# Two attention loops with two step tables: in most groups of the second, VectorE makes 20 of 64 score tiles instead of 19

## The chip, the cores and the metric

The kernel runs on one core of a Trainium2 chip. The metric is the device time of one execution in microseconds (us), taken over several runs. A profile of one execution shows what each engine of the core does: PE is TensorE (matrix products; PEld is its weight loads), ACT is ScalarE, DVE is VectorE, POOL is GpSimd, SP issues transfers.

## What is computed

Four residual layers, two kinds in turn, on a sequence of 2048 rows of 512 features:

```python
x = x + _A_ref(_layernorm(x), A_w_r, A_w_i)      # filter in the frequency domain
x = x + _B_ref(_layernorm(x), wq, wk, wv, wo)    # attention, 32 heads, one shared key/value head
x = x + _A_ref(...);  x = x + _B_ref(...)        # the same weights once more

# _B_ref:  q = x @ wq (32 heads of 16);  k = x @ wk (16);  v = x @ wv (16)
scores = jnp.einsum("bhqd,bkd->bhqk", q, k) * (Dh ** -0.5)
o = jnp.einsum("bhqk,bkd->bhqd", _softmax(scores), v);  return o @ wo
```

The two attention layers take most of the time. Each has 32 heads x 2048 x 2048 scores, and every score needs an exponential.

## The kernel before

**Groups and tiles.** An attention layer is one loop (`Attention.run`, from L558; it is called twice, once for each "pair" of a filter and an attention layer, L1053). It goes over 32 groups: 4 query blocks of 512 rows, and 8 sets of 4 heads in each. A group has 64 score tiles (16 blocks of 128 keys x 4 heads), each 128 keys x 512 queries. A tile is made by one product with 32 rows of K (`score`, L673).

**Two ways to an exponential.** Most tiles go to ScalarE, which takes the exponential of two or three tiles in one instruction (`act_step`, L764). The others go to VectorE: one instruction a tile (`dv_pass`, L798, "a pass") multiplies and adds, and the 16-bit integer that comes out is read as a bfloat16, a rough power of two. It is made better by three shifted copies of the same integers ("images"), each with its own weight in the values table. Two images are made by VectorE for a whole batch of tiles at a time (`image_step`, L813), the third by GpSimd, one tile at a time (L817). A VectorE tile thus needs four products with the values, a ScalarE tile one (`pv_step`, L777).

**Steps.** The order of all engines is written out by hand as a list of steps; `chain()` keeps each engine to it. A step is one ScalarE instruction: 3 tiles in even steps, 2 in odd ones (`OPW`, L31 and L585). In a group of the loop 19 tiles are VectorE's, in three batches of 6, 7 and 6 (`DPOS`, L28); 45 are ScalarE's, which makes 18 steps. Group 0 has no first batch, so ScalarE makes 51 tiles there. The second loop has 579 steps in all. `s0[g]` is the first step of group g; steps below are counted from it.

**What one step issues**, in this order (L833 to L851): the score products of ScalarE's tiles and the exponential; the score products of VectorE's tiles (one as a rule, two in a doubled step); on VectorE what is pending (the query cast L489 or the residual add L733 behind a product of the step before), the turning of a finished group (L694), the passes, what is due (reciprocal L699, `qabs` L493, the turning back L715), then an image; on GpSimd its images and the division (L709); then the products with the values, up to a number of rounds of four (`ROUNDS`, L656); and last a "piece": the product of the next group's queries (L483) or, in four groups of a query block, a product with `wo` (L728). VectorE's scores have two banks of PSUM; a piece holds one of them until its result is taken. ScalarE's have one buffer of 3 banks and one of 2.

**GpSimd is paced.** Each of its images and each division waits for the VectorE image issued last (`pace`, L679).

The first loop's row statistics (L150) follow its residual adds; in the second loop the finished rows are sent out instead (L1044). The planner's numbers that the change touches are module constants: `DPOS`, `SHORT`, `TWICE`, `IMG`, `ROUNDS`, `QSTEP`, `OSTEP`, `STAT`, `HOLD`, `QABS` (L28 to L32), and the delays in `evict` and `normalise` (1 step to the reciprocal, 3 to the division, 3 from there to the turning back; L699, L700, L723). Both loops use the same.

Of the kernel before, what the change touches and what calls it, by code (L numbers as in the profile page):

```python
# [470 lines left out]
class Attention:  # L471
# [86 lines left out]
    def run(self, row_done, work, psums):  # L558
# [7 lines left out]
        def chain():  # L566
            traced = nc.cur_bb.bb.instructions
            start = 0
            if mark[0] is not None:
                start = next(k for k in reversed(range(len(traced))) if traced[k] is mark[0]) + 1  # L570
                for i in traced[start:]:
# [6 lines left out]
            mark[0] = traced[-1]  # L578

        NG = NQB * HG  # L580
        ops = []
        stream = [(g, p // 4, p % 4) for g in range(NG) for p in range(64)
                  if not any(p in pos for pos in DPOS[g == 0:])]
# [9 lines left out]
        NS = len(ops)  # L593
        d_score, d_phase = {}, {}
        for g in range(NG):
            for b, pos in enumerate(DPOS):
                if g == 0 and b == 0:
                    continue
                base = s0[g] + BSTEPS * b
                tiles = [(p // 4, p % 4) for p in pos]  # L600
                steps = [base - BSTEPS + k for k in range(BSTEPS) for _ in range(1 + (len(pos) > BSTEPS and k in TWICE[b]))]
                clash = lambda pm: sum(any(u[2] == tiles[i][1] for u in ops[n]) for n, i in zip(steps, pm)) + \
                    sum(tiles[i][1] == tiles[j][1] for n, m, i, j in zip(steps, steps[1:], pm, pm[1:]) if n == m)
                pm = min(itertools.permutations(range(len(pos))), key=clash)
                tiles = [tiles[i] for i in pm]
                for i, n in enumerate(steps):
                    d_score.setdefault(n, []).append((g, b, i) + tiles[i])
                for k in range(BSTEPS):
                    d_phase[base + k] = (g, b, k, tiles)
                s1[g] = max(s1[g], base + BSTEPS - 1)  # L610
        LAG, NBT = 2, max(len(pos) for pos in DPOS)
# [17 lines left out]
        piece_at = {}  # L629

        def place(n0, kind, k):
            n = n0 if n0 % 2 else n0 + 3
            piece_at[n] = (kind, k)

        for g in range(NG - 1):
            place(s0[g] + QSTEP, "q", g + 1)
        for qb in range(NQB - 1):
            for i in range(4):
                place(s0[HG * (qb + 1) + 1 + i] + OSTEP, "o", 4 * qb + i)

        def full_round(queue):
            lst = []
# [6 lines left out]
        for n in range(NS + LAG + 2):  # L649
            queue += due.get(n, [])  # L650
            lst = pv_list[n] = []
            if n in evict_at:
                assert not any(u[0] == evict_at[n] for u in queue)
                continue
            g = evict_at.get(n + 1)
            rounds = 0 if n in piece_at else ROUNDS[n % 2]  # L656
            while queue:
                rnd = full_round(queue if g is None or not any(u[0] == g for u in queue) else [u for u in queue if u[0] == g])
                must = g is not None and any(u[0] == g for u in queue)
                if not must and (rounds <= 0 or len(rnd) < 4 and len(queue) < HOLD):  # L660
# [29 lines left out]
        def evict(g):  # L690

            ps = pv.pop(g)
            o = small.tile([P, 16, 32], F32, tag="oraw")
            nc.vector.transpose(out=o.rearrange("p c j -> p (c j)"), in_=ps)  # L694
# [36 lines left out]
        def residual(k, ps):  # L731
            r, t = (k % 4, k // 4)
            nc.vector.tensor_tensor(out=x_sb[:, r, t, :], in0=ps, in1=x_sb[:, r, t, :], op=ALU.add)  # L733
            if t == NQB - 2:
                n = s0[NG - 3 + r // 2] + (4, 14)[r % 2]
            else:
                n = s0[HG * (t + 1) + 5 + r] + STAT
            later(max(2, n - now[0]), lambda: finish(r, t))

        def finish(r, t):  # L740
# [60 lines left out]
        def image_step(n):  # L801
            if n in d_phase:
                g, b, k, tiles = d_phase[n]
                src, nt = tb[(g, b)].bitcast(I16), len(tiles)
                if k == 0:
                    pool_new = work.tile([P, NBT, 512], I16, tag="SP", bufs=2)
                    sb[(g, b, 3)] = pool_new
                if k in IMG:
                    i = 1 + IMG.index(k)
# [3 lines left out]
                    image[0] = nc.vector.tensor_scalar(out=s_new[:, lo:nt, :], in0=src[:, lo:nt, :], scalar1=PH_OFF[i], scalar2=None, op0=ALU.add)  # L813
                    if lo:
                        pace(nc.gpsimd.tensor_scalar(out=s_new[:, 0:lo, :], in0=src[:, 0:lo, :], scalar1=1.0, scalar2=PH_OFF[i], op0=ALU.mult, op1=ALU.add))
# [4 lines left out]
        def piece(kind, k):  # L820
            ps = psd.tile([P, 512], F32, tag=f"dv{1 - bank[0]}")
            held[0] = ps
            if kind == "q":
                qproj(k, ps)
                pending.append(lambda: QT.__setitem__(k, qcast(ps)))
                later(QABS, lambda: qabs(QT[k]))
            else:
                outproj(k, ps)
                pending.append(lambda: residual(k, ps))
            pending.append(lambda: held.__setitem__(0, None))  # L830

        pending = []
        for n in range(NS + LAG + 2):  # L833
            now[0] = n
            act_step(n)
            dv = dv_score(n)
            for fn in pending:
                fn()
            del pending[:]
# [38 lines left out]
def full_kernel(ctx, tc, A_x, A_w_r, A_w_i, B_x, B_wq, B_wk, B_wv, B_wo, out, n_pairs=2):  # L878
# [135 lines left out]
    for pair in range(n_pairs):  # L1014
# [35 lines left out]
        with ExitStack() as ap:  # L1050
            work = ap.enter_context(tc.tile_pool(name=f"workB{pair}", bufs=2, side="right", reuse_waits="tile"))
            psums = [ap.enter_context(tc.tile_pool(name=f"{n}{pair}", bufs=1, space=PSUM, reuse_waits="tile")) for n in ("psc", "psd", "psp")]
            last = att.run(row_done, work, psums)  # L1053
# [62 lines left out]
```

## Time and profile before

| | us |
|---|---|
| three runs, median (lowest to highest) | 1527.45 (1525.3 to 1530.04) |
| the profiled execution's own time | 1530.11 |
| its span, first to last instruction | 1528.3 |
| first loop, window 107 to 757: DVE, ACT, PE, POOL busy, of 650.0 | 622.02, 646.87, 579.85, 377.17 |
| between the loops, window 757 to 857: DVE, ACT, PE busy, of 100.0 | 90.74, 62.49, 89.81 |
| second loop, window 857 to 1520: DVE, ACT, PE, POOL busy, of 663.0 | 623.62, 658.01, 590.23, 386.43 |

The profile gives an engine's busy time as a union: where two instructions of one engine overlap, the time counts once. A row of its time line reads: start, time, engine, line, operation, result <- inputs, shapes, and how many instructions were merged; in brackets the idle time before it and what ended it. L813 with 128x3072 is an image of six tiles, with 128x3584 one of seven. On VectorE and ScalarE an instruction starts before the one ahead has ended, so what an instruction costs in a full queue is the distance from its start to the next one's, and not its own length.

### The profile page before, as it was taken

How to read it: one execution, taken by the hardware profiler on the slowest of the kernel's cores; microseconds unless marked ns; L12 is line 12 of the kernel's file. 1: busy time of each engine (PE TensorE's matmuls, PEld its weight loads, DVE VectorE, ACT ScalarE, POOL GpSimd, SP SyncE). 2: the span in 40 equal slices, each digit the busy share in tenths (PEclk: the TensorE clock that was granted, in tenths of full speed). 3: DMA queues.
4: the chain of work that ended last, by engine and by line, in shares of the span. 5: the costliest groups of instructions: out<-in, count | busy, mean ns of one | idle time of the engine just before them, and what ended most of it. 6: DMA issues, size and time to landing. Idle time of an engine off the chain costs nothing.

```text
span 1528.3 us, 32995 instructions
## 1 busy us (share of the span) xinstructions
PE 1345.2 (88%) x13152; PEld 427.7 (28%) x13192; DVE 1429.0 (94%) x2283; ACT 1427.3 (93%) x1349; POOL 781.0 (51%) x1310
## 2 busy tenths in 40 slices
PE   5988888899889988999889888889998899889987
PEld 2532222222222222222235322222222222222222
DVE  7888999999999999999989789999999999999996
ACT  4669999999999999999964899999999999999997
POOL 1005555555556555655600155555556655665555
PEclk9988999999999999999999899999999999999999
DMA  8120000000000000000010100000000000000000
GB/s 286 25 42 2 1 2 2 2 1 2 2 2 2 1 2 2 1 2 1 2 47 13 23 2 2 1 2 5 5 2 5 5 5 5 5 5 5 5 5 18
DMA packets 25263, 20.69 MB, mean 14 GB/s; under 512 B 17428, under 2 KB 22548, under 8 KB 24852
## 3 DMA queue, kind: packets, MB, share of 16 engines
q1 hardware_dynamic: 24724, 17.53, 3.9%
q8 instruction: 103, 1.69, 0.5%
q0 software_dynamic: 384, 1.05, 0.2%
q14 instruction: 52, 0.43, 0.1%
HBM read 13.59 MB, written 2.10 MB: 10 GB/s over the span
## 4 chain that ended last, share of the span: by engine, by line
DVE 35%; ACT 34%; issue 14%; PE 11%; POOL 0%; DVEq 0%; POOLq 0%; ACTq 0%
ACT e L764 34%; DVE t_new L798 17%; DVE s_new L813 9%; PE sc L675 3%; PE pv_new L777 3%; DVE o L694 1%; DVE qt L489 1%; DVE ot_new L715 1%; PE dv L675 1%; DVE st L159 1%; PE new L271 1%; PE new L441 1%; DVE qt L493 1%; DVE x_sb L457 0%; PE new L411 0%
## 5 line engine op out<-in xcount | busy, mean ns | idle before, releaser
L764 ACT ACTIVATE e<-sc 128x1536 bf16<-128x1536 f32 (+1 forms) x1158 | 1314.1, 1301 | 5.7 <-PE dv L675 3.6
L817 POOL TENSOR_SCALAR pool_new<-t_new 128x512 int16<-128x512 int16 x1204 | 730.2, 629 | 707.6 <-DVE s_new L813 614.4
L798 DVE TENSOR_SCALAR t_new<-dv 128x512 uint16<-128x512 f32 x1204 | 789.8, 678 | 58.4 <-PE dv L675 51.4
L777 PE MATMUL pv_new<-e,vaug 128*32 128x512 bf16 x2892 | 587.1, 388 | 0.0
L675 PE MATMUL sc<-qt,KT 32*128 32x512 bf16 x2892 | 457.1, 386 | 115.8 <-ACT e L764 110.5
L675 PE MATMUL dv<-qt,KT 32*128 32x512 bf16 x1204 | 452.7, 386 | 18.9 <-DVE t_new L798 15.8
L777 PE MATMUL pv_new<-s_new,vaug 128*32 128x512 bf16 x2408 | 427.7, 386 | 6.7 <-DVE s_new L813 6.2
L813 DVE TENSOR_SCALAR s_new<-t_new 128x3584 int16<-128x3584 int16 (+1 forms) x380 | 393.5, 1036 | 0.1
L675 PEld LDWEIGHTS <-KT 32*128 32x128 bf16 x4096 | 156.0, 91 | 558.3 <-issue 553.4
L777 PE MATMUL pv_new<-pool_new,vaug 128*32 128x512 bf16 x1204 | 301.5, 384 | 1.4 <-POOL pool_new L817 1.4
L777 PEld LDWEIGHTS <-vaug 128*32 128x32 bf16 x7708 | 156.1, 94 | 381.3 <-issue 349.9
L777 PE MATMUL pv_new<-t_new,vaug 128*32 128x512 bf16 x1204 | 232.1, 387 | 0.3
L483 PE MATMUL ps<-xz,wq_sb 128*128 128x512 bf16 x248 | 65.2, 385 | 0.9 <-DVE t_new L798 0.8
L271 PE MATMUL new<-tab_F,xz 128*128 128x512 bf16 x187 | 45.8, 385 | 7.1 <-DVE xz L235 6.9
L694 DVE STREAM_TRANSPOSE o<-pv_new 128x512 f32<-128x512 f32 x64 | 45.3, 707 | 7.3 <-PE pv_new L777 7.3
L489 DVE TENSOR_SCALAR qt<-ps,kq 128x512 bf16<-128x512 f32 x62 | 46.0, 742 | 1.2 <-PE ps L483 1.2
L186 ACT ACTIVATE X_new<-x_sb,ln_nb,ln_rstd 128x512 bf16<-128x512 bf16 x43 | 33.0, 807 | 8.5 <-DVE ln_nb L171 6.1
L709 POOL TENSOR_TENSOR od_new<-o,den 128x256 bf16<-128x256 f32 x62 | 38.6, 622 | 0.0
L159 DVE BATCH_NORM_STATS2 st<-x_sb 128x6 f32<-128x512 bf16 x52 | 33.6, 678 | 3.7 <-DMA x_sb<-in_A_x_dram 3.5
L483 PEld LDWEIGHTS <-wq_sb 128*128 128x128 bf16 x256 | 22.1, 97 | 32.2 <-issue 17.1
L166 ACT ACTIVATE ln_rstd<-ln_mv,ln_eps 128x4 f32<-128x4 f32 (+1 forms) x15 | 4.5, 297 | 26.5 <-DVE ln_mv L163 26.5
L195 ACT CAST x_new<-new 128x1024 bf16<-128x1024 f32 x12 | 12.1, 1012 | 16.9 <-PE new L309 15.5
(117 smaller groups left out, 597.6 us busy)
## 6 DMA issues: line engine op xcount, KB each, us to landing
tab_F<-const_F SPq DMA_DIRECT2D x5, 640.0 KB, 8.6
t_new<-const_IE SPq DMA_DIRECT2D x2, 1024.0 KB, 6.9
x_sb<-in_A_x_dram SPq DMA_DIRECT2D x3, 512.0 KB, 6.9
rt<-in_A_w_r_dram SPq DMA_DIRECT2D x1, 1028.0 KB, 8.3
rt<-in_A_w_i_dram SPq DMA_DIRECT2D x1, 1028.0 KB, 6.5
t_new<-const_IO SPq DMA_DIRECT2D x2, 512.0 KB, 4.2
out_dram<-x_sb SPq DMA_DIRECT2D x8, 128.0 KB, 1.8
out_dram<-x_sb POOLq DMA_DIRECT2D x8, 128.0 KB, 2.2
```

What stands on the lines that cost most here:

```text
L159: self.nc.vector.bn_stats(st, x_t[:, r, :])
L271: self.mm(ps, lhsT=z, rhs=tab, start=start and i == 0, stop=stop and i == len(mms) - 1)
L483: self.nc.tensor.matmul(ps, lhsT=self.aw["wq"][:, c, hg, :], rhs=self.xT[:, 4 * qb:4 * qb + 4, c, :], start=(c == 0), stop=(c == NC - 1))
L489: self.nc.vector.tensor_scalar(out=qt, in0=ps, scalar1=self.kq[:, 1:2], scalar2=None, op0=ALU.mult)
L675: nc.tensor.matmul(dst, lhsT=KT[hs, kc * P:(kc + 1) * P], rhs=QT[g][hs, :], start=True, stop=True)
L694: nc.vector.transpose(out=o.rearrange("p c j -> p (c j)"), in_=ps)
L709: return engine.tensor_tensor(out=turned_od[g // 2][:, :, half], in0=o[:, :, 0:DH], in1=den.unsqueeze(2).broadcast_to([P, 16, DH]), op=ALU ...
L764: nc.scalar.activation(out=e[:, 0:na, :], in_=sc[:, 0:na, :], func=ACT.Exp, scale=SCALE)
L777: nc.tensor.matmul(pv[g][32 * h:32 * h + 32, :], lhsT=vaug[:, max(j, 0), kc, :], rhs=rhs, start=(first_pv[(g, h)] == u), stop=(last_pv[(g, ...
L798: nc.vector.tensor_scalar(out=tb[(g, b)][:, i, :], in0=dv, scalar1=T_MUL, scalar2=T_ADD, op0=ALU.mult, op1=ALU.add)
L813: image[0] = nc.vector.tensor_scalar(out=s_new[:, lo:nt, :], in0=src[:, lo:nt, :], scalar1=PH_OFF[i], scalar2=None, op0=ALU.add)
L817: pace(nc.gpsimd.tensor_scalar(out=sb[(g, b, 3)][:, i, :], in0=src[:, i, :], scalar1=1.0, scalar2=PH_OFF[3], op0=ALU.mult, op1=ALU.add))
```

## The change

The module constants become a table `LOOPS`, with one entry for each loop, and `run` is handed the pair's number. The first entry has the old numbers, and its plan has kind N (6, 7, 6 tiles) in all groups. The second entry has kind A (7, 7, 6) in 20 groups and kind N in the 12 groups 9 to 12, 17 to 20 and 25 to 28; the products with `wo` are issued in those twelve.

```diff
-DPOS = ((1, 4, 8, 11, 15, 18), (21, 24, 27, 30, 33, 36, 39), (44, 47, 51, 54, 58, 61))
-SHORT = -1
-TWICE, IMG = ((0,), (0,), (0,)), (0, 3)
+DPOS = ({6: (1, 4, 8, 11, 15, 18), 7: (1, 4, 7, 10, 13, 16, 19)},
+        {7: (21, 24, 27, 30, 33, 36, 39)},
+        {6: (44, 47, 51, 54, 58, 61)})
+KINDS = {"N": (6, 7, 6), "A": (7, 7, 6)}
+LOOPS = (dict(PLAN="NNNNNNNNNNNNNNNNNNNNNNNNNNNNNNNN",
+               SHORT=14, IMG=((0, 3), (0, 3), (0, 3)),
...
+               RCP=1, NRM=3, TRN=3, TFIRST=(), ROUNDS=(2, 4), QSTEP=7, QABS=1, OSTEP=13, STAT=14, HOLD=8),
+         dict(PLAN="AAAAAAAAANNNNAAAANNNNAAAANNNNAAA",
+               SHORT=14, IMG=((0, 4), (1, 2), (0, 2)),
+               DK={(0, 6): (0, 1, 2, 3, 4, 5), (0, 7): (0, 1, 2, 2, 3, 4, 5), (1, 7): (0, 0, 1, 2, 3, 4, 5), (2, 6): (0, 1, 2, 3, 4, 5)},
+               RCP=2, NRM=4, TRN=6, TFIRST=(), ROUNDS=(4, 4), QSTEP=5, QABS=1, OSTEP=13, STAT=14, HOLD=8))
-ROUNDS, QSTEP, OSTEP, STAT, HOLD, QABS = (2, 4), 7, 13, 14, 8, 1
...
-            w = OPW[len(ops) % 2] - (len(ops) % 18 == SHORT)
+            w = OPW[len(ops) % 2] - (tiles == 20 and n == C["SHORT"] + (begun[g] + C["SHORT"]) % 2)
...
-                steps = [base - BSTEPS + k for k in range(BSTEPS) for _ in range(1 + (len(pos) > BSTEPS and k in TWICE[b]))]
+                steps = [base - BSTEPS + k for k in C["DK"][b, len(pos)]]
...
-            later(1, lambda: nc.vector.reciprocal(out=den, in_=o[:, :, DH]))
-            later_pool(3, lambda: normalise(g, o, den))
+            later(C["RCP"], lambda: nc.vector.reciprocal(out=den, in_=o[:, :, DH]))
+            later_pool(C["NRM"], lambda: normalise(g, o, den))
...
-                later(3, lambda: turned_back(g))
+                later(C["TRN"], lambda: turned_back(g))
```

`TFIRST` is empty in both entries, so the branch that the diff adds for it in the loop over steps is not taken. A group of kind A has 44 tiles for ScalarE. It keeps its 18 steps: one step of three tiles becomes one of two (`SHORT`).

What the second entry means for a group of kind A, in steps counted from `s0`:

| | before | after |
|---|---|---|
| VectorE's tiles by batch | 6, 7, 6 | 7, 7, 6 |
| step with two passes | 0 | 0, and 14 (for the next group's first batch) |
| VectorE images of the batches | 0, 3 / 6, 9 / 12, 15 | 0, 4 / 7, 8 / 12, 14 |
| turning of the group before, its reciprocal | 3, 4 | 3, 5 |
| its division on GpSimd, turning back (every second group) | 6, 9 | 7, 13 |
| product of the next queries, cast, `qabs` | 7, 8, 8 | 5, 6, 6 |
| rounds of products with the values, at most, in an even and an odd step | 2, 4 | 4, 4 |
| ScalarE step with a tile less | none | 16 |

The groups of kind N keep their tiles, and have the new steps for all the rest.

More of the change, by code (lines that the diff above doesn't have):

```diff
@@ L556, in ready, with run @@
         nc.vector.tensor_scalar(out=qt, in0=qt, scalar1=kq[:, 1:2], scalar2=None, op0=ALU.mult)
-    def run(self, row_done, work, psums):
+    def run(self, row_done, work, psums, pair):
+        C = LOOPS[pair]
         nc, tc, tabs, x_sb, KT, small = self.nc, self.tc, self.tabs, self.x_sb, self.KT, self.small
@@ L580, in run @@
         NG = NQB * HG
-        ops = []
+        positions = lambda g: [DPOS[b][k] for b, k in enumerate(KINDS[C["PLAN"][g]])]
+        ops, begun = [], {}
         stream = [(g, p // 4, p % 4) for g in range(NG) for p in range(64)
-                  if not any(p in pos for pos in DPOS[g == 0:])]
+                  if not any(p in pos for pos in positions(g)[g == 0:])]
         while stream:
-            w = OPW[len(ops) % 2] - (len(ops) % 18 == SHORT)
+            g = stream[0][0]
+            n = len(ops) - begun.setdefault(g, len(ops))
+            tiles = sum(KINDS[C["PLAN"][g]])
+            w = OPW[len(ops) % 2] - (tiles == 20 and n == C["SHORT"] + (begun[g] + C["SHORT"]) % 2)
             ops.append(stream[:w])
@@ L595, in run @@
         for g in range(NG):
-            for b, pos in enumerate(DPOS):
+            for b, pos in enumerate(positions(g)):
                 if g == 0 and b == 0:
@@ L610, in run @@
                 s1[g] = max(s1[g], base + BSTEPS - 1)
-        LAG, NBT = 2, max(len(pos) for pos in DPOS)
+        LAG, NBT = 2, max(max(KINDS[k]) for k in C["PLAN"])
         evict_at = {s1[g] + LAG + 1: g for g in range(NG)}
@@ L655, in run @@
             g = evict_at.get(n + 1)
-            rounds = 0 if n in piece_at else ROUNDS[n % 2]
+            rounds = 0 if n in piece_at else C["ROUNDS"][n % 2]
             while queue:
@@ L659, in run @@
                 must = g is not None and any(u[0] == g for u in queue)
-                if not must and (rounds <= 0 or len(rnd) < 4 and len(queue) < HOLD):
+                if not must and (rounds <= 0 or len(rnd) < 4 and len(queue) < C["HOLD"]):
                     break
@@ L825, in piece @@
                 pending.append(lambda: QT.__setitem__(k, qcast(ps)))
-                later(QABS, lambda: qabs(QT[k]))
+                later(C["QABS"], lambda: qabs(QT[k]))
             else:
@@ L836, in run @@
             dv = dv_score(n)
+            if C["TFIRST"] and (n in evict_at and C["TFIRST"][1] or pending and C["TFIRST"][0]):
+                dv_pass(n, dv)
+                dv = []
             for fn in pending:
@@ L1052, in full_kernel @@
             psums = [ap.enter_context(tc.tile_pool(name=f"{n}{pair}", bufs=1, space=PSUM, reuse_waits="tile")) for n in ("psc", "psd", "psp")]
-            last = att.run(row_done, work, psums)
+            last = att.run(row_done, work, psums, pair)
     with tc.tile_pool(name="psE", bufs=4, space=PSUM, reuse_waits="tile") as pse:
```

11 lines of the change are left out of this document (6 added, 5 removed).

## The prediction

> **What bounds the kernel now.** The change touches the second loop alone: the first loop's entry has the old numbers, so I cost the first loop and the filter layers at nothing. I read the busy times by window first, one plain group of the second loop (20.4 us from 943.6) and a stretch with a product with `wo` (from 1085.6):
>
> ```profile
> core 0: us, PE busy (x) PEld busy (x) DVE busy (x) ACT busy (x) POOL busy (x), PEclk, DMA share, GB/s
> 857.00:877.70 20.70, 17.17 (x162) 4.84 (x161) 15.41 (x25) 18.83 (x24) 6.71 (x10) 0.75 0.00 1
> 877.70:898.40 20.70, 18.47 (x166) 4.98 (x165) 17.50 (x28) 19.56 (x19) 9.51 (x16) 0.84 0.01 2
> 943.60:964.00 20.40, 17.83 (x193) 5.30 (x190) 19.48 (x31) 20.40 (x20) 11.94 (x20) 1.00 0.00 1
> 1085.60:1106.00 20.40, 18.97 (x200) 5.36 (x193) 19.77 (x31) 20.33 (x19) 11.94 (x20) 1.00 0.01 3
> ```
>
> ScalarE is busy without a gap; VectorE is 0.9 us short of it, TensorE 2.6 us, and 1.4 where a product with `wo` falls. So ScalarE bounds the loop, by a hair. The first two windows are slower for another reason: the granted TensorE clock is 0.75 and 0.84 there. Next, the groups of instructions in the window of the second loop, for the size of a ScalarE tile:
>
> ```profile
> L764 ACT ACTIVATE e<-sc 128x1536 bf16<-128x1536 f32 x289 | 438.1, 1516 | 2.1 <-PE dv L675 1.6
> L764 ACT ACTIVATE e<-sc 128x1024 bf16<-128x1024 f32 x289 | 316.2, 1094 | 0.5 <-PE dv L675 0.4
> ```
>
> Then the time line of VectorE (and two rows of GpSimd, last) over one group, because what counts is the distance between starts:
>
> ```profile
> 948.96 0.71 DVE L694 STREAM_TRANSPOSE o<-pv_new 128x512 f32<-128x512 f32 x1
> ...
> 953.08 1.08 DVE L813 TENSOR_SCALAR s_new<-t_new 128x3584 int16<-128x3584 int16 x1
> 954.08 0.69 DVE L798 TENSOR_SCALAR t_new<-dv 128x512 uint16<-128x512 f32 x1
> 954.68 0.74 DVE L489 TENSOR_SCALAR qt<-ps,kq 128x512 bf16<-128x512 f32 x1
> 955.34 0.68 DVE L798 TENSOR_SCALAR t_new<-dv 128x512 uint16<-128x512 f32 x1
> 955.93 0.35 DVE L493 TENSOR_SCALAR qt<-qt,tab_QAND 128x512 int16<-128x512 int16 x1
> 956.21 0.68 DVE L798 TENSOR_SCALAR t_new<-dv 128x512 uint16<-128x512 f32 x1
> ...
> 966.07 1.29 DVE L798 TENSOR_SCALAR t_new<-dv 128x512 uint16<-128x512 f32 x2 [0.73 <-PE dv L675]
> 967.27 0.95 DVE L813 TENSOR_SCALAR s_new<-t_new 128x3072 int16<-128x3072 int16 x1
> 968.14 1.28 DVE L798 TENSOR_SCALAR t_new<-dv 128x512 uint16<-128x512 f32 x2
> 969.34 0.71 DVE L694 STREAM_TRANSPOSE o<-pv_new 128x512 f32<-128x512 f32 x1
> ...
> 977.18 1.49 DVE L813 TENSOR_SCALAR s_new<-t_new 128x3584 int16<-128x3584 int16 x1
> 978.59 1.90 DVE L798 TENSOR_SCALAR t_new<-dv 128x512 uint16<-128x512 f32 x3
> ```
> ```profile
> 975.89 0.62 POOL L709 TENSOR_TENSOR od_new<-o,den 128x256 bf16<-128x256 f32 x1
> 976.48 1.25 POOL L817 TENSOR_SCALAR pool_new<-t_new 128x512 int16<-128x512 int16 x2
> ```
>
> The turnings at 948.96 and 969.34 are a group apart: **20.38 us a group**. From start to start a pass costs 0.60, an image of six 0.87, of seven 1.00, the turning 0.63, the cast 0.66, `qabs` 0.28, the turning back 0.62 (956.81 to 957.43) in every second group, the reciprocal 0.15. Where a pass waited 0.73 us, it waited for its scores (PE dv), which stand behind ScalarE's in TensorE's queue: VectorE is held to ScalarE's pace. The image at 977.18 took 1.49 us, its like at 953.08 1.08: GpSimd's second image of the pair at 976.48 was still running, to 977.73. I call such a 0.41 us a **collision**; it happens in every second group, the one without the turning back (in the other the same image, at 957.43, took 1.05).
>
> **The change part by part.** *ScalarE in a group of kind A*: a step of 1516 ns becomes one of 1094, so 20.38 - 0.42 = 19.96 us. That is the floor, and there are as many steps as before. *VectorE*: before, 19 x 0.60 + 4 x 0.87 + 2 x 1.00 + 0.63 + 0.15 + 0.66 + 0.28 + half of 0.62 = 18.91, and half a collision, 19.1 of 20.38. After, 20 passes (12.0), four images of seven (4.00), two of six (1.74), and the same 2.03: **19.77 without collisions**. So VectorE gains 0.86 us of work while ScalarE loses 0.42, and the two end 0.19 apart: a collision of 0.41 decides which sets the pace.
>
> *Collisions after* are worked out from these distances and from GpSimd's (an image each 0.585, as 1.79 for three; first start 0.1 to 0.2 after the image that releases it). Step 7 to 8: the images of the second batch are one pass apart, 1.60 from start to start; GpSimd is released at 1.08 and its image runs from about 1.2 to 1.8, across the start: some 0.1 to 0.2 lost. Step 8 to 12: GpSimd has the division and four images (2.9 us) behind the second one, VectorE four passes; the next image starts at 3.40, near the boundary of two GpSimd instructions: nothing or 0.4. Step 6: `qabs` comes 3.0 us after the image of step 4, while GpSimd works off four images (1.2 to 3.5): nothing or 0.4. At the others GpSimd is done before. Bounds 0.1 and 1.0 (three places); I take **one full collision a group**, since one place costs less than that and two are even. That gives VectorE 19.77 + 0.41 = 20.18, above ScalarE's 19.96: the pace of a group of kind A is 20.18, 0.20 less than now.
>
> *Can they be that close without waiting for each other?* The heaviest stretch after is steps 6 to 8: cast, pass, `qabs`, pass, image, pass, image are 0.66 + 0.60 + 0.28 + 0.60 + 1.00 + 0.60 + 1.00 = 4.7 us against three ScalarE steps of about 3.6 (20.38 / 18 each, and the 3-2-3 order). VectorE falls back 1.1 us. Before, the row of 954.68 to 958.40 is as heavy (3.7 us in two steps, 2.3), and ScalarE shows no idle time in that window. I cost the coupling at nothing, with a bound in the rivals.
>
> *TensorE*: a tile more on VectorE is three products with the values more, 124 instead of 121, in rounds of four; 0.75 round of 0.22 us (two rounds took 0.61, one 0.39) beside 2.6 us of idle time: nothing. *GpSimd*: one image more, 0.62, beside 8.4 us idle: nothing but the collisions. *The moved reciprocal, division and turning back* are all issued as often as before; the output product that needs the turned values comes in the next query block's groups, many steps later. *Groups of kind N*: the same work; ScalarE's pace, with little room on TensorE (1.4 us). The query product is two steps farther from the `wo` product than before, which can only space them out; more rounds in even steps can delay scores. Bounds -1 and +1 us over the twelve groups; I take 0, as both act on the same queue.
>
> *Sum*: of the 20 groups of kind A I leave out 0 (no first batch) and 1, where the clock is low. 18 x 0.20 = 3.6 us less. The profiled execution would go from 1530.11 (span 1528.3, 1.8 around it) to 1526.5. It lies 2.7 above the median of the three runs, so against the median: 1527.45 - 3.6 = **1523.9**. A difference of 0.3% (4.6 us) is about what a measurement of this kernel can tell from none.
>
> [...]
>
> **Rivals.** 1. *ScalarE gets all of it*: the collisions fall between instructions, and the pace is 19.96. For: 0.19 us of room, and images that start near a GpSimd boundary. Against: two images a single pass apart. 18 x 0.42 = 7.6 us, **1519.9**; with the two first groups and 1 us from kind N, 1518.1. 2. *VectorE with GpSimd becomes a slower bound than ScalarE was* (slower): it decides from 20.38 - 19.77 = 0.61 us of collisions a group on, one and a half full ones. Two in each group: 20.59, +0.21 x 18 = 3.8, **1531.2**; three: 21.00, **1538.6**. For: GpSimd's bursts are longer by an image. 3. *The query product comes late*: before it, in step 4, up to four rounds of products instead of two, 0.44 us, now stand ahead of the next scores. For: TensorE is 17.83 of 20.4 us busy. Against: the 2.6 us that are left. If half of it delays ScalarE in all 31 groups, +6.8 against the gain of 3.6: **1530.7**. 4. *Passes in a full queue cost their own length*, 0.68 (the mean of L798 is 678 ns): VectorE at 19.77 + 20 x 0.08 = 21.37, +0.99 x 18 = 17.8, **1545.3**. Against it stand the three passes from 978.59, done in 1.90; and 19 of them would already have made VectorE the bound before. 5. *The plan has no effect on time* (the tile taken from ScalarE is one that it waited out elsewhere): **1527.5**.
>
> **How the numbers follow.** Forecast (between no more than half a collision lost and one and a half, 1519.9 to 1527.5) 0.50; rival 1 0.18; rival 2 0.15; rival 3 0.08; rival 4 0.03; rival 5 0.06. Faster by over 0.3% (below 1522.9): rival 1 and 0.20 of the forecast, 0.38. Within: 0.30 of the forecast, 0.05 of rival 2, 0.03 of rival 3, and rival 5: 0.44. Slower (above 1532.0): the rest of rivals 2, 3 and rival 4: 0.18. The range goes from rival 1 with all its extras to two full collisions and a little: 1518 to 1532.
>
> **What would show it.** Turnings (L694) 20.1 to 20.3 apart in groups 2 to 8, with ScalarE idle for some 0.2 us a group and VectorE's waits for PE dv nearly gone: the forecast. ScalarE without gaps at 19.96: rival 1. Images of 1.3 us and more twice or three times a group: rival 2. ScalarE's idle time behind PE sc at steps 6 and 7: rival 3. Kind N far from 20.4 to 20.6 would make the sum wrong in a place I costed at nothing.

## The result: 1540.41 us, 0.86% slower

| | before | after |
|---|---|---|
| runs | 4 | 4 |
| median, us (lowest to highest) | 1528.16 (1525.3 to 1530.04) | 1540.41 (1538.48 to 1542.27) |
| profiled execution, its span, us | 1530.11, 1528.3 | 1542.27, 1540.5 |
| second loop, first exponential to the end of the last, us | 659.07 | 671.92 |

The ratio is 1.0086 (95% interval 1.0071 to 1.0101). The forecast was 1523.9, in a range of 1518 to 1532; the kernel became slower, and its time lies above that range. The second loop is 12.85 us longer in the profiled executions, against 12.25 between the medians and 12.2 between the two spans: it holds the whole difference.

Three measures below are worked out from the traces. The **pace** of a group is the distance between the starts of ScalarE instructions 18 steps apart; these stretches begin two steps before `s0`, so the short step 16 of a group of kind A falls into the stretch of the group behind it. The **loss** of a step is the distance between the ends of two successive ScalarE instructions, less what it is in a full queue (1.344 us with three tiles, 0.916 with two); without loss a group of kind N takes 9 x 1.344 + 9 x 0.916 = 20.34 us, one of kind A 19.92. VectorE's **work** in a group is the sum of the distances between its starts, without its idle time.

| us | before | after |
|---|---|---|
| pace, plain groups (2 to 7) | 20.37 | 20.67, 20.49, 20.57, 20.49, 20.58, 20.49 |
| groups with a `wo` product, 10 and 11 | 20.59, 20.41 | 20.69, 20.69 |
| groups 12 / 20 / 28 | 20.59 / 20.59 / 20.59 | **23.87 / 23.86 / 24.08** |
| the groups behind them, 13 / 21 / 29 | 20.32 / 20.32 / 20.32 | 20.76 / 20.76 / 21.58 |
| loss in a plain group | 0.03 | 0.62: steps 1, 6, 7, 12, 16 with 0.04, 0.08, 0.17, 0.19, 0.14 |
| VectorE in a plain group: work, idle | 19.36, 1.01 | 20.25, 0.28 (pace 20.53, mean of groups 4 to 7) |

Groups 12, 20 and 28 and the ones behind them take 3.28 + 0.44 + 3.27 + 0.44 + 3.49 + 1.26 = **12.2 us** more than before. The rest is small and has both signs: plain groups lose 0.1 to 0.3 each, the two first groups gain 1.5 together. About 1 us of that gain isn't the change's: two kernels further down that keep kind N everywhere (`wo` product at step 17; at most two rounds) take 0.98 and 1.10 us less in group 1 than this profile of before, too. The granted clock in the window 880 to 902 was 0.84 in that profile, and 0.92 in those two and in the kernel after.

The groups of instructions of the kernel after, second loop (busy time, mean ns | idle time before them and what ended it):

```profile
L777 ACT ACTIVATE e<-sc 128x1536 bf16<-128x1536 f32 x269 | 399.4, 1485 | 4.7 <-PE dv L688 3.0
...
L777 ACT ACTIVATE e<-sc 128x1024 bf16<-128x1024 f32 x310 | 323.9, 1060 | 12.0 <-PE dv L688 10.2
...
L688 PE MATMUL dv<-qt,KT 32*128 32x512 bf16 x621 | 237.1, 385 | 28.1 <-DVE t_new L811 24.2
```

Before, the row for VectorE's score products was:

```profile
L675 PE MATMUL dv<-qt,KT 32*128 32x512 bf16 x602 | 226.3, 386 | 9.1 <-DVE t_new L798 7.6
```

Twenty steps went from three tiles to two (289 and 289 before, 269 and 310 now; the last step had one tile and has two). But ScalarE now idles 16.7 us ahead of these instructions (2.6 before). In 13.2 us of it a score product for VectorE (PE dv) ended last; it stands in the same queue as ScalarE's own. These products in turn wait 24.2 us for VectorE's passes (t_new), which hold the banks; before, it was 7.6. Two stretches of that kernel by window, a plain group, and the end of group 12:

```profile
core 0: us, PE busy (x) PEld busy (x) DVE busy (x) ACT busy (x) POOL busy (x), PEclk, DMA share, GB/s
...
941.90:962.50 20.60, 18.29 (x196) 4.66 (x192) 20.29 (x31) 20.39 (x19) 13.14 (x21) 1.00 0.00 1
...
1119.40:1124.10 4.70, 4.10 (x38) 1.02 (x32) 4.45 (x8) 4.70 (x6) 3.70 (x6) 1.00 0.00 0
1124.10:1128.30 4.20, 2.76 (x21) 0.63 (x24) 3.32 (x6) 1.46 (x2) 1.09 (x3) 0.75 0.00 0
```

In the plain group VectorE and ScalarE are both nearly full; that is what the forecast wanted. In the 4.2 us from 1124.10 no engine is full: ScalarE is busy for 1.46, TensorE for 2.76, and the granted clock drops to 0.75. The time line of that place:

```profile
1122.64 1.02 PE L741 MATMUL ps<-wo_sb,ot_new 128*128 128x512 bf16 x3
...
1123.99 0.70 DVE L728 STREAM_TRANSPOSE ot_new<-od_new 128x512 bf16<-128x512 bf16 x1
1124.12 0.37 PE L688 MATMUL dv<-qt,KT 32*128 32x512 bf16 x1
...
1124.61 0.65 DVE L746 TENSOR_TENSOR x_sb<-ps,x_sb 128x512 bf16<-128x512 f32 x1
1125.19 0.67 DVE L811 TENSOR_SCALAR t_new<-dv 128x512 uint16<-128x512 f32 x1
1125.91 0.37 PE L688 MATMUL dv<-qt,KT 32*128 32x512 bf16 x1 [1.42 <-DVE t_new L811]
...
1126.21 0.61 PE L790 MATMUL pv_new<-s_new,vaug 128*32 128x512 bf16 x2
...
1128.32 1.02 ACT L777 ACTIVATE e<-sc 128x1024 bf16<-128x1024 f32 x1 [2.76 <-PE dv L688]
```

The `wo` product (step 13) holds one of VectorE's two score banks until the residual add has read it. Group 13 is of kind A, so its first batch has seven tiles, and the doubled step of that batch is step 14 of group 12: the very next one. Its two scores (1124.12 and 1125.91) have to go through the one bank that is left. The second waits for the pass on the first, and that pass stands on VectorE behind the turning back (moved to step 13) and the residual add. TensorE works in the order that `chain()` gives it, so the rounds and ScalarE's scores stand behind it. The products at 1126.21 then take 0.61 each instead of 0.39: the clock has fallen behind the wait (0.50 from 1126.20 to 1129.60). In the like stretches of groups 20 and 28 the granted clock is 0.70 and 0.67; behind the third it is still 0.56 for 4.3 us, which makes group 29 the longest of its kind (21.58).

### The profile page after: what moved, and what is told of

It reads as the page before. It is cut to its first block, busy times and chain, and to the rows that moved or that the text cites. A ratio compares the mean times of both kernels' runs of the same rounds, so it can differ in the third digit from the quotient of the medians.

```text
span 1540.5 us, 33131 instructions
## 1 busy us (share of the span) xinstructions
PE 1357.9 (88%) x13209; PEld 415.0 (27%) x13249; DVE 1447.3 (94%) x2302; ACT 1425.9 (93%) x1349; POOL 808.9 (53%) x1329
## 3 DMA queue, kind: packets, MB, share of 16 engines
q0 software_dynamic: 384, 1.05, 0.2%
## 4 chain that ended last, share of the span: by engine, by line
DVE 53%; ACT 19%; PE 14%; issue 8%; POOL 1%; DVEq 0%; POOLq 0%; ACTq 0%
DVE t_new L811 27%; ACT e L777 18%; DVE s_new L826 16%; PE pv_new L790 4%; PE sc L688 3%; DVE o L707 2%; PE dv L688 2%; DVE qt L501 1%; POOL pool_new L830 1%; DVE qt L497 1%; DVE ot_new L728 1%; DVE st L167 1%; PE new L279 1%; PE new L449 1%; DVE den L712 1%
## 5 line engine op out<-in xcount | busy, mean ns | idle before, releaser
L777 ACT ACTIVATE e<-sc 128x1024 bf16<-128x1024 f32 (+1 forms) x1158 | 1312.8, 1281 | 19.7 <-PE dv L688 14.8
L790 PE MATMUL pv_new<-e,vaug 128*32 128x512 bf16 x2873 | 563.2, 388 | 0.0
L688 PE MATMUL dv<-qt,KT 32*128 32x512 bf16 x1223 | 463.4, 385 | 37.8 <-DVE t_new L811 32.4
L790 PE MATMUL pv_new<-s_new,vaug 128*32 128x512 bf16 x2446 | 395.1, 386 | 4.8 <-DVE s_new L826 4.0
L688 PEld LDWEIGHTS <-KT 32*128 32x128 bf16 x4096 | 147.2, 91 | 563.7 <-issue 558.5
L790 PE MATMUL pv_new<-pool_new,vaug 128*32 128x512 bf16 x1223 | 267.5, 389 | 1.1 <-POOL pool_new L830 1.1
L790 PE MATMUL pv_new<-t_new,vaug 128*32 128x512 bf16 x1223 | 225.0, 390 | 0.3
L722 POOL TENSOR_TENSOR od_new<-o,den 128x256 bf16<-128x256 f32 x62 | 64.2, 1035 | 0.0
L501 DVE TENSOR_SCALAR qt<-qt,tab_QAND 128x512 int16<-128x512 int16 x64 | 33.7, 526 | 0.0
```

The source lines that it names most:

```text
L501: self.nc.vector.tensor_scalar(out=qt.bitcast(I16), in0=qt.bitcast(I16), scalar1=self.tabs["QAND"][:, 0:1], scalar2=None, op0=ALU.bitwise_and)
L688: nc.tensor.matmul(dst, lhsT=KT[hs, kc * P:(kc + 1) * P], rhs=QT[g][hs, :], start=True, stop=True)
L722: return engine.tensor_tensor(out=turned_od[g // 2][:, :, half], in0=o[:, :, 0:DH], in1=den.unsqueeze(2).broadcast_to([P, 16, DH]), op=ALU ...
L777: nc.scalar.activation(out=e[:, 0:na, :], in_=sc[:, 0:na, :], func=ACT.Exp, scale=SCALE)
L790: nc.tensor.matmul(pv[g][32 * h:32 * h + 32, :], lhsT=vaug[:, max(j, 0), kc, :], rhs=rhs, start=(first_pv[(g, h)] == u), stop=(last_pv[(g, ...
```

## The experiments

All kernels are run beside the kernel before, and a ratio is to that kernel, with its interval. Edits are to the second loop's entry of the kernel after, and shown by the values that matter; "old steps" stands for the first entry's `IMG`, `RCP`, `NRM`, `TRN`, `ROUNDS` and `QSTEP`, with `DK[0, 7] = (0, 0, 1, 2, 3, 4, 5)` (doubled step 12 of the group before). "17 A" is the plan with 13, 21 and 29 of kind N, which leaves 17 groups of kind A.

### The long step

**Theory**: the doubled step beside the held bank. **Rival**: the new steps make the groups with a `wo` product slow, whatever the kind of the next group.

```diff
-PLAN="AAAAAAAAANNNNAAAANNNNAAAANNNNAAA"
+PLAN="AAAAAAAAANNNNNAAANNNNNAAANNNNNAA"
```

> The changed kernel with groups 13, 21 and 29 of the second loop as kind N, so that no doubled step of VectorE's scores falls on step 14 of a group with a wo product. Theory (the doubled step needs two banks while the wo product holds one of the two): the three steps of 4.2 us go, 3 x (3.3 + 0.45) = 11 us of the 12 us lost come back, 1529 us. Rival (the groups of kind A are slower everywhere, by 0.15 us each): three groups fewer bring 0.5 us, 1540. Rival (the switch from N to A itself): the 4.2 us steps move to groups 13, 21 and 29, 1540.

Measured: 1531.07 us, 1.0029 (1.0017 to 1.0041). The long steps are gone (group 12 takes 20.69), and 9.3 us with them, though three groups fewer have the extra tile. The theory holds for this part; some 3.7 us stay, where the 1529 expected would have left under 2.

```diff
-(0, 7): (0, 1, 2, 2, 3, 4, 5)
+(0, 7): (0, 1, 2, 3, 3, 4, 5)
```

> The changed kernel with all 20 groups of kind A; only the doubled step for the first batch of seven moves from step 14 to step 15, where the bank of the wo product is free again. Theory (two scores in one bank behind the residual add): no step of 4.2 us is left, 1528 to 1531 us. Rival (the wo product's step is simply overfull on TensorE, with twelve products with the values in step 14): the steps stay long, 1537 or more.

Measured: 1541.48, 1.0090 (1.0074 to 1.0105). The long step is gone (group 12 loses 1.06 instead of 3.53), but the doubled step now stands close to the next group's own doubled step 0: groups of kind A go from 20.53 to 20.85 and 20.68. Two groups, 15 and 31, take 21.95 and 22.53, as the granted clock falls in them (0.51 in the 3.5 us from 1174.50, 0.50 in the 4.0 us from 1507). The place was right, the total missed.

```diff
-OSTEP=13
+OSTEP=15
```

> The changed kernel with the wo products two steps later (step 15 instead of 13), so that their bank is held in step 16, the doubled step staying at 14. Theory (held bank and doubled step together): the 4.2 us steps go, 1528 to 1531 us. Rival (any wo product in a group that feeds kind A): 1537 or more.

Measured: 1539.68, 1.0076 (1.0060 to 1.0093). Again the long step is gone (loss 1.52 in group 12), and the held bank does harm elsewhere: 21.24 and 20.82 in groups 10 and 11, 21.23 in group 13. The total missed.

```diff
-PLAN="AAAAAAAAANNNNAAAANNNNAAAANNNNAAA", OSTEP=13
+PLAN="NNNNNNNNNNNNNNNNNNNNNNNNNNNNNNNN", OSTEP=17
```

> The kernel before, except that the wo products of the second loop come at step 17 instead of 13, so that their bank is held in the next group's step 0, which has always had two passes. No group of kind A, none of the new steps. Theory (held bank and doubled step together): twelve stalls of 2 to 3.5 us, 24 to 42 us slower than before, 1552 to 1570. Rivals (new steps, or kind A, as the cause): within 5 us of before.

Measured: 1536.71, 1.0059 (1.0044 to 1.0074). This one has the old steps. With the tiles and steps of before and the `wo` product just ahead of a doubled step (0 of the next group), there are twelve stalls, in the twelve places; each costs 0.7 to 0.9 (21.25 instead of 20.32 to 20.59). So a held bank beside a doubled step does cost by itself, while the size expected (2 to 3.5 each) was missed by far. It costs a quarter of the 3.3: here no turning back stands ahead on VectorE, and the clock stays (1.00 from 1070 to 1100, over such a group), though TensorE waits 1.05 us for t_new each time.

```diff
-TRN=6
+TRN=3
```

> The changed kernel (all its stalls in place) with the turning back three steps after the division, as before, instead of six, so that it no longer stands on VectorE ahead of the residual add of the held bank. Theory (the 4.2 us step is a chain on VectorE: turning back, residual add, pass, score, pass; and TensorE waits so long that its clock falls to half): 0.6 us less ahead of the chain, no fall of the clock, the step shrinks to 2.5 to 3 us, 1534 to 1537 us. Rival (only the held bank counts): the step stays above 3.8, 1539 to 1541.

Measured: 1533.90, 1.0050 (1.0036 to 1.0064). 6.5 us come back. Groups 12, 20 and 28 take 22.07, 23.36 and 22.07, with the same wait of TensorE in all three (0.83 us for t_new, where it was 1.42). Windows of the stall in group 12 and in group 20 of this run tell them apart:

```profile
1119.60:1123.60 4.00, 3.01 (x27) 0.84 (x30) 3.54 (x6) 2.57 (x3) 1.21 (x2) 1.00 0.00 0
1285.50:1290.10 4.60, 3.60 (x27) 0.86 (x30) 3.89 (x7) 2.49 (x3) 1.38 (x3) 0.81 0.09 29
```

The clock (the column after POOL) stays at 1.00 in the first and falls to 0.81 in the second. So the fall costs 23.36 - 22.07 = **1.3 us**, the turning back ahead 23.87 - 23.36 = **0.5** (both with the fall), and the bank with the residual add 22.07 - 20.59 = **1.5**: the 3.3 us of a long step. The split is an estimate from single places. The 1.5 holds some 0.3 of the new steps (group 10, which has no long step, takes 20.87 in this run, 20.59 before). And the turning back has a part in the fall, too: with it ahead the clock fell in three places of three, without it in one of three.

```diff
-TFIRST=()
+TFIRST=(1, 0)
```

> The changed kernel, but behind a piece VectorE's passes come ahead of the residual add or the query cast. Theory (in the doubled step two scores go one after the other through one bank, and the residual add stands ahead of the first pass): the 4.2 us steps shrink by 0.6 to 1.5 us, 1535 to 1539 us; they do not go, as the bank is still held. Rival (the residual add has no part in it): 1540 to 1542.

Measured: 1560.29, 1.0215 (1.0198 to 1.0232). With the pass ahead of what is pending, the long step shrinks from 4.22 to 2.69 us, about as expected. The clock stays at 1.00 in groups 12 and 20; in group 28 it falls (0.56 in the 4.5 us from 1479.0), behind waits of 0.82 and 0.30 us. But the query cast now stands behind a pass too, so its bank is held longer: ScalarE loses 0.76 us at step 8 in 18 groups, and 0.33 to 0.65 in the twelve of kind N. The total is a plain miss, and a second sign of what a held bank costs.

### Why a plain group of kind A takes 20.5 and not 20.2

Theory at first: VectorE's own sum, with its collisions, sets the pace. Rivals: the new steps cost it, or TensorE's queue.

```diff
-PLAN="AAAAAAAAANNNNAAAANNNNAAAANNNNAAA"
+PLAN="NNNNNNNNNNNNNNNNNNNNNNNNNNNNNNNN"
```

> The changed kernel's new steps with no tile moved: all 32 groups of the second loop of kind N. Theory (VectorE is the bound only in groups of kind A; the new steps add a 0.4 us wait of qabs for GpSimd, which kind N has room for): within 2 us of before, 1526 to 1529. Rival (the new steps themselves cost 0.15 us in every group): 1531 to 1533.

Measured: 1532.74, 1.0034 (1.0021 to 1.0047). The new steps without the extra tile cost 5 us: little in plain groups (20.42, loss 0.08), but 0.44 at step 15 of each group with a `wo` product (20.85). Less what those twelve groups lost before (0.07 or 0.25), that is some 4 of the 5 us. The rival was right in the total, not in the place. Why step 15 loses there I did not separate (turning back, `wo` product and images are all near).

```diff
-IMG=((0, 4), (1, 2), (0, 2)), RCP=2, NRM=4, TRN=6, ROUNDS=(4, 4), QSTEP=5
+IMG=((0, 3), (0, 3), (0, 3)), RCP=1, NRM=3, TRN=3, ROUNDS=(2, 4), QSTEP=7
```

> The changed kernel's tiles (20 groups of kind A) with the old steps for images, queries, reciprocal, division, turning back and rounds; the doubled step of a first batch of seven is step 12, two steps before the one in which the wo product holds a bank. Theory (held bank and doubled step made the three 4.2 us steps; collisions and the step table decide the rest): no such step, VectorE 19.8 plus half a collision in kind A, pace 20.0 to 20.3, 1522 to 1526 us. Rival (a twentieth tile does not fit, whatever the steps): above 1529.

Measured: 1529.55, 1.0013 (1.0003 to 1.0022). With the old steps and 20 groups of kind A, these go at 20.38 and 20.31: VectorE's work is 20.16, but ScalarE loses 0.39 at step 10 in each of them, so the tile's 0.42 is given back at one step. Groups 12, 20 and 28 take 21.39, 0.8 more than before. The total is where the rival had it; a kernel further down shows that the tile does fit.

```diff
-PLAN="AAAAAAAAANNNNAAAANNNNAAAANNNNAAA", QABS=1
+PLAN="AAAAAAAAANNNNNAAANNNNNAAANNNNNAA", QABS=2
```

> As e1_three_n (groups 13, 21 and 29 of kind N), and qabs one step later, where GpSimd's burst is over. Theory (qabs waits 0.39 us for GpSimd in every group, and VectorE sets the pace of kind A): 0.2 to 0.4 us less in 16 groups, 1525 to 1528 us. Rival (VectorE and ScalarE wait for each other through TensorE's queue, and the collision lies in that wait): at most 1 us less, 1530 to 1531.

Measured: 1530.18, 1.0019 (1.0010 to 1.0028). The collision at `qabs` is gone and VectorE's work falls from 20.25 to 19.98. The pace hardly follows (20.53 to 20.49), and VectorE's idle time grows from 0.28 to 0.5. So VectorE's sum doesn't set the pace with the new steps: my theory falls, the rival stands.

```diff
-PLAN="AAAAAAAAANNNNAAAANNNNAAAANNNNAAA"
+PLAN="ANANANANANNNNNANANNNNNANANNNNNAN"
```

> The old steps, and kind A in ten groups only, none next to another and none that feeds a held bank (0, 2, 4, 6, 8, 14, 16, 22, 24, 30). Theory (VectorE has about 20.2 us of work in kind A and 19.1 in kind N, against ScalarE's 19.96 and 20.38: only a neighbour of kind N gives room for the tile): ScalarE keeps the pace of both kinds, 10 x 0.4 = 4 us less than before, 1523 to 1524.5. Rival (VectorE and ScalarE stop each other within a few steps, and room in the next group does not help): 1527 to 1529.

Measured, with the old steps: 1529.23, 1.0013 (1.0004 to 1.0023). Each group of kind A still loses 0.39 at step 10, with neighbours that lose 0.06. What is lost is lost inside the group; that the neighbour gives room falls.

```diff
-IMG=((0, 4), (1, 2), (0, 2))
+IMG=((0, 3), (0, 4), (0, 3))
```

> The old steps, kind A in the 17 groups of e1_three_n, and the second image of the middle batch one step later (step 10 instead of 9), away from the cast, qabs and turning back. In e6_tiles_alone ScalarE lost 0.39 us in each group of kind A at one place, behind steps 8 and 9. Theory (the loss is that pile on VectorE within three steps, not its sum over the group): pace of kind A 20.0 to 20.1, 1522 to 1525 us. Rival (VectorE's sum, 20.16 and a little idle time): pace 20.3, 1526 to 1528.

Measured, with 17 A and for the rest the old steps: 1533.30, 1.0044 (1.0031 to 1.0057). The loss at step 10 stays at 0.39, and one of 0.4 to 0.5 comes up at step 12 of the groups with a `wo` product. So it isn't the image at step 9, and the rival's time was missed as well.

The time lines ahead of step 10 then showed the cause. Before (group 5; the scores of ScalarE's steps 9 and 10, and ScalarE's row, in which nothing waits):

```profile
972.00 5.69 ACT L764 ACTIVATE e<-sc 128x1024 bf16<-128x1024 f32 x5
...
976.04 0.39 PE L675 MATMUL sc<-qt,KT 32*128 32x512 bf16 x2
...
977.12 0.39 PE L675 MATMUL sc<-qt,KT 32*128 32x512 bf16 x3
```

The same steps with the extra tile (20 A, old steps):

```profile
973.77 0.39 PE L688 MATMUL sc<-qt,KT 32*128 32x512 bf16 x2
...
975.07 0.39 PE L688 MATMUL sc<-qt,KT 32*128 32x512 bf16 x3
...
975.56 1.45 ACT L777 ACTIVATE e<-sc 128x1536 bf16<-128x1536 f32 x1 [0.28 <-PE dv L688]
```

From the scores of step 9 to those of step 10 it is 1.08 us before and 1.30 with the tile. Between them lie the rounds of step 9: 11 products in three rounds before, 15 in four now, as the tile's products fill a round. Step 8 had already run late: VectorE's score waited 0.23 and 0.25 us there for the one bank that the query product leaves. So these 0.22 us had no slack, and ScalarE idles. New theory: **the rounds that stand behind the query product in TensorE's queue**.

```diff
-ROUNDS=(4, 4)
+ROUNDS=(2, 4)
```

> As e1_three_n, with two rounds of products with the values in an even step instead of four. Theory (VectorE's order of images and passes makes ScalarE lose 0.6 us a group, at steps 7, 12 and 16): no change beyond 1 us, 1530 to 1532. Rival (the third of the prediction: up to four rounds ahead of the query product make the scores late): the loss at steps 6 and 7 goes, 0.2 us in 30 groups, 1524 to 1526.

Measured, with 17 A and the new steps: 1530.71, 1.0023 (1.0014 to 1.0033). The losses at steps 6, 7 and 12 are gone or small, and 0.38 comes up at step 8: step 7, the first step with four rounds behind the query product, now has 16 products. It moves with the rounds, as the rival has it; no time is won, as the theory had it for another reason.

Three kernels with the old steps and 17 A, alike but for the rounds in odd steps (four, three and two), and a control with kind N in all groups and two rounds. The last of the three is

```diff
-PLAN="AAAAAAAAANNNNAAAANNNNAAAANNNNAAA", ROUNDS=(4, 4)
+PLAN="AAAAAAAAANNNNNAAANNNNNAAANNNNNAA", ROUNDS=(2, 2)
```

beside the old `IMG`, `DK`, `RCP`, `NRM`, `TRN` and `QSTEP`.

> Control: the old steps with kind A in 17 groups (not 13, 21, 29, which feed a group with a wo product's held bank). As e6_tiles_alone, where ScalarE lost 0.39 us at step 10 of each group of kind A, without that kernel's 0.9 us in each of groups 12, 20 and 28. All theories: 1525.5 to 1528 us, the loss at step 10 still there.

> As e14_old_steps_17, with at most three rounds of products with the values in an odd step instead of four, so that step 9 has three as it had before the twentieth tile. Theory (the loss at step 10 is TensorE's: held bank, then a round too many ahead of ScalarE's scores): it falls from 0.39 to about 0.15, 1522 to 1525 us. Rival (VectorE's sum of 20.2 us sets the pace of kind A): pace 20.3 still, within 1 us of e14.

> As e14_old_steps_17, with at most two rounds in any step, so that step 9 has two. Theory (TensorE's rounds behind the query product): the loss at step 10 goes below 0.1 us, pace of kind A 20.0 to 20.1, 1520 to 1523 us, unless the products put off to step 2 (six rounds there in groups with a wo product) cost it back. Rival (VectorE's sum): pace 20.2 to 20.3, at most 2 us less than e14.

> Control: the kernel before (kind N and the old steps everywhere) with at most two rounds in any step of the second loop. All theories: ScalarE had no loss to give back in kind N (0.03 us a group), so within 1.5 us of before, 1526 to 1529.

| | us | ratio | plain groups | loss in a plain group |
|---|---|---|---|---|
| 17 A, (2, 4) | 1527.33 | 0.9998 (0.9988 to 1.0007) | 20.37 and 20.30 | step 10: 0.39 |
| 17 A, (2, 3) | 1523.30 | 0.9974 (0.9965 to 0.9983) | 20.34 and 20.14 | step 10: 0.18, step 13: 0.02 and 0.21 |
| 17 A, (2, 2) | **1522.75** | **0.9969 (0.9958 to 0.9981)** | 20.33 and 20.14 | step 13: 0.39 and 0.19 |
| all N, (2, 2) | 1526.44 | 0.9994 (0.9984 to 1.0003) | 20.34 | none |

The loss at step 10 follows the number of rounds in step 9 (four, three, two): the theory holds for the old steps. The groups with a `wo` product, of kind N, show the same behind that product: with three, four, three and two rounds in step 15 (before, and the three kernels) group 10 loses 0.17, 0.39, 0.18 and nothing at step 16.

What is left is at step 13, more of it in the group with the turning back. From three rounds to two the loss at step 10 goes, and the pace of plain groups stays: what is won at one step is lost at the other. In the group with the turning back VectorE works without a gap ahead of step 13. So the pace expected from the theory (20.0 to 20.1) did not come; the rival's did (20.2 to 20.3).

Rounds alone bring nothing that can be told from no change, and the tile alone neither; together they bring 4.5 us. That kernel beats both. Only a part comes from plain groups: going from (2, 4) to (2, 2) saves 0.04 us in one with the turning back and 0.16 in one without, but 0.43 in each of groups 8, 16 and 24 and 0.15 to 0.27 in each of the groups 9 to 12 and their like (13, 21 and 29 give back 0.13). Its plain groups take 20.24 on the average, of which VectorE works 20.10 and idles 0.14: here at last the pace is close to VectorE's sum, and near the number that the forecast had (20.18). Its stretches at the border to kind N (8 and 9) take 19.90 and 19.88, which is ScalarE's floor.

```diff
-PLAN="AAAAAAAAANNNNAAAANNNNAAAANNNNAAA", ROUNDS=(4, 4)
+PLAN="AAAAAAAAANNNNNAAANNNNNAAANNNNNAA", ROUNDS=(2, 2)
```

> The change's own steps with the plan of the three moved groups (13, 21, 29 of kind N) and at most two rounds of products with the values in every step. Theory (what a group of kind A loses beyond VectorE's sum, it loses because the rounds behind the query product stand in TensorE's queue ahead of ScalarE's next scores): the losses at steps 6 and 7, seen with four rounds in even steps, and the one at step 8, seen with four in odd steps, are both gone; the pace of a group of kind A falls from 20.53 to VectorE's own sum, 20.25 to 20.3 us, as a collision at qabs is left in every group; some 17 x 0.25 = 4.3 us less than the run with the moved groups: about 1526.5 us. Rival (the loss belongs to the new steps of the query product and qabs, whatever the rounds are): the pace stays at 20.5 and the time at 1530 to 1531 us.

Measured, with the new steps: 1535.20, 1.0056 (1.0042 to 1.0070), slower than with four rounds; neither theory nor rival gave that. The loss in plain groups is 0.87, now 0.12, 0.18, 0.40 and 0.14 at steps 0, 7, 12 and 16. The time line of that kernel ahead of the one at step 12, the largest:

```profile
974.68 1.87 DVE L811 TENSOR_SCALAR t_new<-dv 128x512 uint16<-128x512 f32 x3
...
975.41 0.37 PE L688 MATMUL dv<-qt,KT 32*128 32x512 bf16 x1 [0.40 <-DVE t_new L811]
...
976.26 0.39 PE L688 MATMUL sc<-qt,KT 32*128 32x512 bf16 x3
...
976.75 1.45 ACT L777 ACTIVATE e<-sc 128x1536 bf16<-128x1536 f32 x1 [0.30 <-PE dv L688]
```

VectorE works without a gap from 967.8 to 976.55 (cast, `qabs`, two images one pass apart, all between passes); its pass at 974.68 is late, the score at 975.41 waits 0.40 for its bank, ScalarE's scores at 976.26 stand behind that, and ScalarE idles 0.30. With the new steps, then, there is a second hold-up beside the rounds: VectorE's dense stretch. That taking the rounds away only brings ScalarE to it sooner is my reading, and no run shows it. A kernel that cures both with the new steps was not tried, so how much of the 0.6 a group belongs to each stays open.

## Why the prediction was wrong

**Right.** ScalarE bounded the loop before, and a tile is worth 0.42 us of its time. VectorE's sum in a group of kind A was forecast at 19.77 and one collision of 0.41, 20.18; its work is 20.25. Some luck is in that: by the same prices the sum before was 19.1, and its work was 19.36. The one collision is at `qabs` ("nothing or 0.4"), in every group (VectorE's and GpSimd's rows of the kernel after):

```profile
970.77 2.36 POOL L830 TENSOR_SCALAR pool_new<-t_new 128x512 int16<-128x512 int16 x4 [1.03 <-DVE s_new L826]
...
972.55 0.73 DVE L501 TENSOR_SCALAR qt<-qt,tab_QAND 128x512 int16<-128x512 int16 x1
...
974.96 0.62 POOL L830 TENSOR_SCALAR pool_new<-t_new 128x512 int16<-128x512 int16 x1 [1.82 <-DVE s_new L826]
...
975.39 1.12 DVE L826 TENSOR_SCALAR s_new<-t_new 128x3584 int16<-128x3584 int16 x1
...
975.54 1.45 POOL L722 TENSOR_TENSOR od_new<-o,den 128x256 bf16<-128x256 f32 x1
```

`qabs` takes 0.73 (0.35 before), with GpSimd at the last of its four images until 973.13 (the row at 970.77). The images one pass apart lost 0.05 and not 0.1 to 0.2: the second, at 975.39, started 0.18 ahead of the end of GpSimd's image of 974.96, and it was GpSimd's division that took longer (1.45, 0.62 before). Rivals 2 and 4 did not come about.

**Wrong, for 12.2 of the 12.85 us:** "*Groups of kind N*: the same work ... Bounds -1 and +1 us over the twelve groups; I take 0". The work of a group is indeed the same, but its step 14 issues the doubled scores of the *next* group, of kind A, right behind the `wo` product's bank, and the turning back had been moved ahead of them. I had the three facts (doubled step 14, product at 13, turning back at 13) in the table of steps and didn't lay them beside each other; I looked at the queue of products and not at the two banks. Each such place costs 3.3 us: by the estimate above 1.5 the bank and the residual add, 0.5 the turning back, 1.3 the clock. The other groups of kind N were not free either: groups 9, 10 and 11 lose 0.28, 0.35 and 0.35, where they lost 0.07, 0.25 and 0.07.

**Wrong, for what the tile should have brought:** "I cost the coupling at nothing". The prediction let VectorE's sum set the pace of kind A, 20.18; the pace is 20.53, and ScalarE waits for late scores at single steps. A group of kind A loses 0.62 over ScalarE's floor. As an account of VectorE's time that is 20.25 - 19.92 = 0.33 of work and 0.28 of idle time; it is not a split by cause, since with `qabs` a step later 0.27 of the work went and the pace fell by 0.04. The forecast gain of 0.20 a group became a loss of 0.16 (20.53 against 20.37). Without the long steps the loop came out 12.85 - 12.2 = 0.7 us longer, and not 3.6 shorter: 4.3 us, and more without the 1 us of the first groups that isn't the change's. The run without long steps (17 A) shows it directly, at 3.7 us slower than before. The evidence that I took for slack ("as heavy ..., and ScalarE shows no idle time in that window") was a place with none left: with the old steps, one round more there cost 0.39 at once. "0.75 round of 0.22 us ... beside 2.6 us of idle time: nothing" set a local cost against a sum over the whole group. Rival 3 had the engine and the place about right (late scores around the query product, from the rounds), and its 0.22 is near the 0.25 that steps 6 and 7 lose. But its price is fixed; the runs show one that goes from step to step as the table does, and is gone from step 10 with two rounds and the old steps. That its 1530.7 lies near the run without long steps (1531.07) is luck: with two rounds in even steps the loss at steps 6 and 7 all but goes, and the time stays (1530.71).

The chances fail for the same reason: 0.18 for slower came from rivals with their causes in plain groups alone, and none looked at the border between two kinds.

## What to carry to other kernels

When work is moved in a table that an in-order queue follows, compare step by step what holds a shared buffer and what stands ahead of the instruction that frees it, above all where two kinds of group meet and the earlier one issues work of the later one. A sum over a group, and idle time averaged over it, say nothing of the one step that has no slack. And a saved instruction pays only if the queue that feeds the saving engine is thinned at that place too: here the tile and the rounds bring 4.5 us together, and alone nothing that can be told from no change.

## What the runs showed of the hardware

- **The clock fell after a wait of 1.42 us.** The product of 0.37 at 1125.91 is followed by one of 0.61 at 1126.21, in a window with a granted clock of 0.75. In another kernel (turning back early) the same wait of 0.83 us left the clock at 1.00 in two places and lowered it in a third (0.81). Nor does the longest single wait decide it: the waits of 1.05 us with the `wo` product at step 17 left it at 1.00 (1070 to 1100), and in the kernel with the doubled step at 15 it fell to 0.51 behind waits of 0.65, 0.41 and 0.49 within 5 us. In the kernel after, the three falls behind the long steps lasted 3.4, 3.4 and 6.5 us from the first slow product to the first fast one (from 1126.21, 1293.47 and 1461.04). What decides whether the clock falls, and for how long, no run here shows.
- **VectorE and GpSimd held each other up.** `qabs` took 0.73 with 0.58 left of GpSimd's running image, and lost 0.38. The VectorE image at 975.39 lost 0.05 with 0.18 left of GpSimd's, and GpSimd's division, next in its queue, took 0.83 longer. In these two places VectorE lost less than what was left of the instruction that GpSimd was running, and did not wait for those queued behind it (the division in the second).
